# A hand-ordered two-layer Hedgehog attention and ReGLU prompt kernel on one core: a new order, queues for the first loads, transposes in transpose mode, and a last tile split 384 and 128

## The chip, the cores and the metric

The kernel runs on one core of one Trainium2 chip. The metric is the device time of one execution in microseconds (us). Before the change it is 376.75 us, the median of 3 runs (376.38 to 376.97).

Five engines take part, each with its own instruction stream and semaphores between them: TensorE (PE) for matrix products, VectorE (DVE), ScalarE (ACT), GpSimd (POOL), and SyncE (SP), which here only issues DMA transfers. ACT can issue transfers too. An engine takes its own instructions in the order in which they were written down, and stands still when the next one's data are not there.

## The reference

`x` has 2048 rows of 512. Two blocks, A (linear attention, 32 heads of 16) and B (a gated feed-forward of width 1376), are applied twice with the same weights:

```python
def A(x):                                   # B=1, S=2048, D=512, H=32, Dh=16
    q, k, v = split_heads(x @ wqkv)
    pq, pk = q @ w_phi, k @ w_phi           # per head, 16x16
    phi_q = concat(softmax(pq), softmax(-pq))
    phi_k = concat(softmax(pk), softmax(-pk))
    kv, z = phi_k.T @ v, phi_k.sum(over s)
    o = (phi_q @ kv) / (phi_q @ z + 1e-6)
    return merge_heads(o) @ wo
def B(x):
    gate, up = x @ W_gate, x @ W_up
    return (relu(gate) * up) @ W_down
x = x + A(layernorm(x)); x = x + B(layernorm(x))     # twice
```

Everything is bfloat16 outside, with 32-bit sums inside.

## The kernel before

The 2048 rows are 16 tiles of 128. `w_phi` is folded into the key and query weights at the start: a weight is turned on PE (`turn`, L444) or by DMA (L439), multiplied by a block-diagonal matrix (`fold`, L452), and cast back to SBUF (`Wk2`, `Wq2`).

Per tile and layer the attention block does this. `stats` (DVE, L481), `ln` (ACT, L489, function Ln) and `rstd` (ACT, L491, function Exp) make the row scale. The scaled tile is turned, by PE and a cast or by a DMA transpose. `K` (PE, L539) is four products of 128x512 into a PSUM tile `b`, of which there are six. Two `ek` (ACT, L542, Exp) take it out with both signs. `sk` (DVE, L550) sums the heads, `lnk` (ACT, L559, Ln) and `rk` (ACT, L562, Exp) turn the sums into reciprocals, and two `phi` (L513, POOL or DVE) scale. `V` (PE, L545) and its cast `vext` give the values, and `kvz` (PE, L574) adds the tile's part to the sums over all rows. Queries go the same way: `Q` (PE, L601), two `Eq` (ACT, L604, Exp), `sq` (DVE, L607), `lnq` (ACT, L612, Ln), `rq` (ACT, L614, Exp), a scaling, and a DMA transpose `fq`.

When all 16 `kvz` of a layer are in, `R` (DVE, L586 and L591) is built from the sums. Only then can the first `erq` (PE, L638) of the layer run, which makes a tile's attention output; after it come `o`, its turn, `proj` (L661) and the residual. The feed-forward takes blocks of one to four tiles: `G` and `Up` (L738), ACT's relu (L742), the product `hT`, `down` (L778) and the residual (L785). The tail of 96 columns of the width goes through L714. The last tile of layer 1 is stored in two column halves.

The order isn't made by a scheduler on the spot. The program builds 1880 `Op` objects; `ORDER`, a list written out by hand or by a search before, says in which sequence they are emitted, `SLOTS` which buffer each takes, `PLACE` which of two engines an op with an alternative goes to, and `IDLE` how many filler products on zeros stand before which PE op. Each engine's stream is its share of that sequence. `arrange` asserts that an op's `deps` have been emitted before it; what an op has in `follow` is not asserted.

One ACT op matters by its place alone. Op 2, named `tbl`, emits `preload_act_table_set("natural_log_exp_and_others")`: a load of the activation table set that holds both Ln and Exp. No op has it in its `deps`, and it has the load before it in `follow` only. When the program is built, an ACT function that isn't in the set loaded last in the stream gets a load of a set put in before it.

The first transfers of `x` and the weights are bound to a queue in the code, two to ACT and the others to SP. At the very start PE multiplies zeros (`warm`, L423): eight products of 128x512.

Of the kernel before, what the change touches and what calls it, by code (L numbers as in the profile page):

```python
# [8 lines left out]
P = 128  # L9
D = 512  # L10
# [3 lines left out]
NB = D // P  # L14
NF = 11
FR = F - (NF - 1) * P
T = 16
C = 4
# [124 lines left out]
class K:  # L143
# [9 lines left out]
    "0101010100000000001100000001110000101110000110101000000100000101000000010000100000011000000011101010"  # L153
    "1010011010111000101011000001100011100001011100000101101000111000000011000111010011000001101100001011"
    "0110101011100110011100010111110101000100110000001000001100000111100100010000110001001001011010111001"
    "010000101101110101001101111111110"
)
SLOTS = (
    "0011432021055021001401501045313321124221352412451013e0315g31303b0305c12201i012432332391030654220f321"
    "4h220030344d100111082247052a331k1615010b1250052c1344300g0132252j045e363d1200040401141402000224011020"  # L160
    "0400001134021012100000203101002122001002541105001002511102104910002413114215400412511651100100120031"
    "1420302310051535031h432112311505010425412301310405420324310022031410j5100a24022k02327101200410401103"
    "12242250121002352020511310154521505223522020e4231c031213111011021411125513140225000g3420030030020120"
    "03413125121121433231f0121f214i00181651332422193104055j333k204b360a2243033d242h304i113805010401021210"
    "0000121002100010010021140010123402000043001010020111302020011511301002431321101003205504010521311411"
    "5402110501523540013000121032150140030110232043213110025124210401311015522400200403422412313320414041"
    "210100300531330452512524210005215103213300111020141500412"
)
IDLE = (
    0, 0, 0, 1, 0, 0, 0, 0, 0, 0, 1, 0, 1, 0,  # L170
# [105 lines left out]
def kernel(  # L276
# [73 lines left out]
    def load_x(t, n, due, follow=(), eng="SP"):  # L350
        o = load(due, X[t // C][:, t % C:t % C + n, :], xv[:, t:t + n, :], n * 131072, eng, follow)
        x_in[t:t + n] = [o] * n
# [438 lines left out]
    p = PAR  # L791
# [103 lines left out]
```

## Time and profile before

| | |
|---|---|
| time, median of 3 runs | 376.75 us (376.38 to 376.97) |
| the profiled execution's own time | 376.44 us |
| its span, first to last instruction | 374.7 us |
| PE busy | 363.8 us (97%) |
| DVE busy | 275.9 us (74%) |
| ACT busy | 204.3 us (55%) |
| POOL busy | 80.4 us (21%) |
| ACT table loads | 1, of 1283 ns |

The span lies between the first and the last instruction; the execution's own time is 1.7 us longer. "Busy" is the union of an engine's instructions in time. Consecutive ACT instructions overlap, so the step from one start to the next is shorter than an instruction's own duration, and an engine whose instructions start in such steps without a pause has none to spare. Matmuls are pipelined as well.

### The profile page before, as it was taken

To read this page: it belongs to the slowest core of one execution; us is meant where nothing else is said; L and a number is where in the kernel's file an instruction comes from. 1 tells how busy PE (TensorE), PEld (TensorE's weight loads), DVE (VectorE), ACT (ScalarE), POOL (GpSimd) and SP (SyncE) were. 2 spreads that over 40 slices of the span, in tenths; PEclk is the share of its full clock that TensorE was granted. 3 is DMA by queue.
4 is the path that set the end of the run, shared out by engine and by line. 5 is a ranking of instruction groups with operands and counts; after the bars stand their busy time and mean duration, and the time that the engine had idled before them with its cause. 6 is when DMAs were issued, how large, how long until landed. Compare 5 with 4: busy or idle time off the path is not lost.

```text
span 374.7 us, 7403 instructions
## 1 busy us (share of the span) xinstructions
PE 363.8 (97%) x2784; PEld 216.1 (58%) x2830; DVE 275.9 (74%) x587; ACT 204.3 (55%) x561; POOL 80.4 (21%) x93
## 2 busy tenths in 40 slices
PE   7998999999999999999999999999999999999996
PEld 3453455867544544466566456587764444457674
DVE  6999999998775956864789989998776365134333
ACT  5998999655545546344539666874434423313111
POOL 0286985430101100110033533241100000000000
PEclk9999999999999999999999999999999999999999
DMA  8997439875532233042212100488753302020221
GB/s 233 204 232 195 131 81 175 142 142 112 96 59 54 44 65 63 1 84 52 42 38 48 36 0 3 85 115 121 147 94 79 57 0 58 0 56 2 69 74 42
DMA packets 93443, 31.20 MB, mean 83 GB/s; under 512 B 85248, under 2 KB 92384, under 8 KB 93408
## 3 DMA queue, kind: packets, MB, share of 16 engines
q1 hardware_dynamic: 92992, 30.34, 40.1%
q8 instruction: 22, 0.36, 0.4%
q10 hardware_dynamic: 416, 0.39, 0.4%
q14 instruction: 13, 0.11, 0.1%
HBM read 7.91 MB, written 2.10 MB: 27 GB/s over the span
## 4 chain that ended last, share of the span: by engine, by line
PE 89%; issue 1%; ACT 0%; DVE 0%; DVEq 0%
PE b L738 37%; PE b L778 20%; PE b L661 7%; PE b L601 6%; PE b L545 6%; PE b L539 5%; PE b L714 3%; PE q L638 2%; PE q L574 2%; PE b L470 1%; ACT ek L604 0%; DVE o L652 0%; DVE X L785 0%; DVEq L890 0%; ACT lnA L489 0%
## 5 line engine op out<-in xcount | busy, mean ns | idle before, releaser
L738 PE MATMUL b<-xnTB,wgu 128*128 128x128 bf16 (+2 forms) x1200 | 154.5, 279 | 0.2 <-ACT rd L649 0.2
L738 PEld LDWEIGHTS <-wgu 128*128 128x128 bf16 x1200 | 97.5, 98 | 47.3 <-DMA xnTB<-xn 0.4
L742 ACT ACTIVATE gu<-b 128x512 bf16<-128x512 f32 (+1 forms) x83 | 47.2, 581 | 84.8 <-PE b L738 82.0
L778 PE MATMUL b<-wd,hT 128*128 128x512 bf16 (+2 forms) x342 | 83.9, 372 | 0.9
L513 POOL TENSOR_TENSOR ek<-ek,sk 128x512 bf16<-128x512 bf16 x43 | 46.7, 1107 | 122.6 <-ACT sk L562 121.7
L778 PEld LDWEIGHTS <-hT 128*128 128x128 bf16 (+1 forms) x363 | 34.7, 98 | 34.2 <-DVE hT L746 0.2
L755 DVE TENSOR_TENSOR hT<-gu,b 128x512 bf16<-128x512 bf16 (+1 forms) x47 | 30.8, 666 | 30.2 <-ACT gu L742 16.4
L607 DVE TENSOR_REDUCE sq<-ek 128x64 f32<-128x1024 bf16 x32 | 38.4, 1210 | 3.6 <-ACT ek L604 3.5
L604 ACT ACTIVATE ek<-b 128x512 bf16<-128x512 f32 x64 | 37.0, 606 | 6.9 <-PE b L601 6.7
L542 ACT ACTIVATE ek<-b 128x512 bf16<-128x512 f32 x64 | 36.8, 623 | 6.6 <-PE b L539 6.6
L550 DVE TENSOR_REDUCE sk<-ek 128x64 f32<-128x1024 bf16 x32 | 38.2, 1205 | 1.8 <-ACT ek L542 1.8
L785 DVE SCALAR_TENSOR_TENSOR X<-b,rsB,X 128x512 bf16<-128x512 f32 (+1 forms) x33 | 23.9, 729 | 21.2 <-PE b L778 21.0
L757 ACT CAST gu<-b 128x512 bf16<-128x512 f32 (+1 forms) x36 | 20.5, 569 | 25.9 <-PE b L738 25.7
L539 PE MATMUL b<-Wk,xnTA 128*128 128x512 bf16 x122 | 32.2, 379 | 1.1 <-DMA xnTA<-xn 0.6
L545 PE MATMUL b<-wv,xnTA 128*128 128x512 bf16 x124 | 31.8, 379 | 1.3 <-ACT ek L604 1.0
L661 PE MATMUL b<-wo,oT 128*128 128x512 bf16 x121 | 31.5, 379 | 0.4
L622 POOL TENSOR_TENSOR ek<-ek,sq 128x512 bf16<-128x512 bf16 x24 | 25.3, 1060 | 30.4 <-DVE rsB L701 14.3
L601 PE MATMUL b<-Wq,xnTA 128*128 128x512 bf16 x121 | 30.8, 379 | 0.4
L665 DVE SCALAR_TENSOR_TENSOR X<-b,X 128x512 bf16<-128x512 f32 x32 | 22.0, 686 | 9.8 <-PE b L661 9.4
L652 DVE TENSOR_TENSOR o<-q,rd 128x512 bf16<-128x512 f32 x32 | 22.0, 687 | 2.8 <-PE b L738 1.2
L481 DVE BATCH_NORM_STATS2 bstA<-X 128x6 f32<-128x512 bf16 x32 | 21.1, 681 | 2.0 <-DMA X<-in_A_x_dram 1.8
L746 DVE TENSOR_TENSOR hT<-gu 128x512 bf16<-128x512 bf16 (+1 forms) x36 | 15.2, 424 | 10.1 <-ACT gu L757 10.0
(74 smaller groups left out, 351.0 us busy)
## 6 DMA issues: line engine op xcount, KB each, us to landing
out_dram<-X SPq DMA_DIRECT2D x15, 128.0 KB, 1.8
X<-in_A_x_dram SPq DMA_DIRECT2D x6, 256.0 KB, 4.5
wgu<-in_B_W_up_dram SPq DMA_DIRECT2D x4, 344.0 KB, 3.5
wgu<-in_B_W_gate_dram SPq DMA_DIRECT2D x4, 344.0 KB, 4.7
wd<-in_B_W_down_dram SPq DMA_DIRECT2D x5, 256.0 KB, 3.4
wv<-in_A_wqkv_dram SPq DMA_DIRECT2D x2, 256.0 KB, 4.4
wo<-in_A_wo_dram SPq DMA_DIRECT2D x4, 128.0 KB, 3.5
fq<-ek SPq DMA_TRANSPOSE x32, 3.3
```

The source lines that it names most:

```text
L513: e.tensor_tensor(out=out().rearrange("p g s (h f) -> p (g s h) f", f=DH)[:, lo:lo + n], in0=ek.t[:].rearrange("p g s (h f) -> p (g s h) f ...
L539: k = op("PE", mm(4, 512), due, lambda: [nc.tensor.matmul(kp.t[:], lhsT=xnTA[c][:, i, b, :], rhs=Wk2[:, b, :], start=(b == 0), stop=(b == ...
L542: e = [op("ACT", act(512), due, lambda s=s: nc.scalar.activation(out=ek.t[:, :, s, :], in_=kp.t[:].rearrange("p (g e) -> p g e", e=GQ), fu ...
L545: v = op("PE", mm(4, 512), due_v, lambda: [nc.tensor.matmul(vp.t[:], lhsT=xnTA[c][:, i, b, :], rhs=wv[:, b, :], start=(b == 0), stop=(b == ...
L550: a = op("DVE", SUM16, due, lambda: nc.vector.tensor_reduce(out=sk.t[:, row, :], in_=ek.t[:].rearrange("p g s (h f) -> p (g s h) f", f=DH) ...
L601: q = op("PE", mm(4, 512), due, lambda: [nc.tensor.matmul(qp.t[:], lhsT=xnTA[c][:, i, b, :], rhs=Wq2[:, b, :], start=(b == 0), stop=(b == ...
L604: e = [op("ACT", act(512), due, lambda s=s: nc.scalar.activation(out=ek.t[:, :, s, :], in_=qp.t[:].rearrange("p (g e) -> p g e", e=GQ), fu ...
L607: a = op("DVE", SUM16, due, lambda: nc.vector.tensor_reduce(out=sq.t[:], in_=ek.t[:].rearrange("p g s (h f) -> p (g s h) f", f=DH), axis=A ...
L661: a = op("PE", mm(4, 512), due + 3, lambda j=j, yp=yp: [nc.tensor.matmul(yp.t[:], lhsT=oT.t[:, j, b, :], rhs=wo[:, b, :], start=(b == 0), ...
L738: nc.tensor.matmul(ps.t[:, q * W:(q + 1) * W].rearrange("p (i t) -> p i t", t=P), lhsT=wgu[:, s, b, g * P:(g + 1) * P], rhs=xT.t[:, 0:n, b ...
L742: nc.scalar.activation(out=gu.t[:, 0, 0:cols], in_=gp.t[:, 0:cols], func=AF.Relu)
L778: nc.tensor.matmul(yp.t[:, 0:c1 - c0], lhsT=h.t[:m, f * W + i * P:f * W + (i + 1) * P], rhs=wd[:m, f, c0:c1], start=(f == 0), stop=(f == N ...
```

## The change

- `ORDER`, `SLOTS`, `PLACE` and `IDLE` are new throughout. `IDLE` has two filler products, not three.
- `warm` is seven zero products, not eight.
- The loads of `x`, of the key and value weights and of `w_phi` get an alternative: ACT or SP may issue them, as `PLACE` says. ACT now issues five, SP 28 of the loads (before: two and 31).
- The turns on PE, which were products with the identity into 32-bit PSUM, are transposes (`nc.tensor.transpose`) into the same PSUM tile read as bfloat16; the cast that takes them out reads bfloat16.
- The last tile of layer 1 is split into 384 and 128 columns, not 256 and 256.

```diff
-    0, 0, 0, 1, 0, 0, 0, 0, 0, 0, 1, 0, 1, 0,
+    0, 0, 0, 2, 0,
...
-    0, 4, 21, 18, 24, 3, 2, 16, 7, 26, 8, 17, 1, 22, 23, 29, 25, 9, 10, 46, 14, 19, 47, 27, 48, 322, 49, 30, 32, 31,
+    16, 7, 8, 17, 29, 24, 18, 22, 4, 3, 21, 19, 23, 20, 26, 322, 0, 1, 10, 324, 64, 82, 65, 323, 83, 66, 27, 30, 67,
...
+    228, 366, 204, 180, 229, 282, 182, 239, 454, 298, 165, 181, 230, 240, 232, 2, 241, 308, 169, 341, 455, 244, 345,
...
-    def load(due, dst, src, nbytes, eng="SP", follow=()):
-        q = nc.sync if eng == "SP" else nc.scalar
-        return op(eng, dma(nbytes), due, lambda: q.dma_start(out=dst, in_=src), name="load", follow=follow,
-                  move=nbytes / RATE)
+    def load(due, dst, src, nbytes, eng="SP", follow=(), both=False):
+        queues = {"SP": nc.sync, "ACT": nc.scalar}
+        ways = {e: (e, dma(nbytes), lambda q=q: q.dma_start(out=dst, in_=src), False) for e, q in queues.items()}
+        return op(eng, dma(nbytes), due, ways[eng][2], name="load", follow=follow, move=nbytes / RATE,
+                  alt=ways["ACT" if eng == "SP" else "SP"] if both else None)
...
-    op("PE", mm(8, 512), 0, lambda: idle(8), [c_z], [wps], name="warm")
+    op("PE", (2570, 2700, 6), 0, lambda: idle(7), [c_z], [wps], name="warm")
...
+    def half(ps):
+        return ps.t[:].bitcast(BF16)[:, 0:NB * P]
...
-        a = op("PE", mm(NB, 128), due, lambda: [nc.tensor.matmul(
-            ps.t[:, b * P:(b + 1) * P], lhsT=src.t[:, 0, b * P:(b + 1) * P], rhs=ident[:], start=True, stop=True)
-            for b in range(NB)], after + [c_id], [ps], [src], name=name)
+        a = op("PE", mm(NB, 128), due, lambda: [nc.tensor.transpose(
+            half(ps)[:, b * P:(b + 1) * P], src.t[:, 0, b * P:(b + 1) * P], ident[:]) for b in range(NB)], after + [c_id], [ps], [src], name=name)
...
-            halves = ((0, 256), (256, 512)) if l == 1 and t == T - 1 else ((0, 512),)
+            halves = ((0, 384), (384, 512)) if l == 1 and t == T - 1 else ((0, 512),)
```

In the list `ORDER`, op 2 (`tbl`) stands at index 6 before and at index 310 after. The ACT stream that is built from the two lists begins like this; the first column is the place in the stream, and lines are those of each kernel's own file (the new file's are two to three higher):

```
before                                            after
1  L346 DMACopy X_61<-in_A_x_dram                 1  L346 DMACopy X_61<-in_A_x_dram
2  L371 LoadActFuncSet                            2  L346 DMACopy hT_162<-in_A_wqkv_dram
3  L346 DMACopy hT_162<-in_A_wqkv_dram            3  L346 DMACopy X_61<-in_A_x_dram
4  L489 Activation lnA_90<-mvA_88,eps             4  L346 DMACopy hT_162<-in_A_wqkv_dram
5  L491 Activation rsA_89<-lnA_90                 5  L346 DMACopy X_62<-in_A_x_dram
6  L429 TensorCopy hT_163<-b_102                  6  L492 LoadActFuncSet
7  L429 TensorCopy hT_163<-b_103                  7  L492 Activation lnA_90<-mvA_88,eps
8  L489 Activation lnA_90<-mvA_88,eps             8  L494 LoadActFuncSet
9  L429 TensorCopy Wk_67<-b_104                   9  L494 Activation rsA_89<-lnA_90
10 L491 Activation rsA_89<-lnA_90                 10 L492 LoadActFuncSet
11 L429 TensorCopy hT_163<-b_105                  11 L492 Activation lnA_90<-mvA_88,eps
12 L429 TensorCopy hT_163<-b_106                  12 L494 LoadActFuncSet
```

Over the whole stream there is 1 `LoadActFuncSet` before and there are 37 after: 36 in front of a Ln or an Exp that is the first or follows one of the other function, and `tbl` itself (L372) at place 143, behind which there is none. Ahead of the first `erq` of layer 0 both PE streams hold the same groups: 16 `K`, 16 `V`, 12 `Q`, 16 `kvz`, four turned tiles, and the turning and folding of the key and query weights. ACT's share ahead of the last `vext` of that layer is the same too, but for three fewer casts of turned tiles (`xnTA`), one fewer of the turned key weight (`wT`), two more of `vext` and one `lnq` fewer; DVE has those turned by ACT before.

More of the change, by code (lines that the diff above doesn't have):

```diff
@@ L152 @@
 PLACE = (
[L153 to L156, printed above, removed]
+    "0010001001000000111010110001000001110000000110000000110000100010000101100010101001000000000000010110"
+    "0101000001110111111111001000010011000001010100001110111011000010011011000110010110101011010110100111"
@@ L157 @@
+    "1101001110110010011001100011000010011111000100101010001000001101010010000001111001000101101100011000"
+    "101111000111110001100001000000001101111110100001"
 )
 SLOTS = (
-    "0011432021055021001401501045313321124221352412451013e0315g31303b0305c12201i012432332391030654220f321"
-    "4h220030344d100111082247052a331k1615010b1250052c1344300g0132252j045e363d1200040401141402000224011020"
-    "0400001134021012100000203101002122001002541105001002511102104910002413114215400412511651100100120031"
@@ L162 @@
[L162 to L166, printed above, removed]
@@ L167 @@
-    "210100300531330452512524210005215103213300111020141500412"
+    "0011432514255040001232121002134310233320053302731103e4125f44110b0334c11110i0305j54121a5200950225h223"
+    "204020413546005k014d1254232834251541365b1133202a061732362402223g011e33091500030401111002000251011020"
+    "1300001130021000330210021402100221010011450404004005114325001c22002012111014324215200h10310500400402"
+    "03045014110422k322504412111115032111121232033043150230033254111530124311284420053302b223001510103000"
+    "21311411232012240050421222251431275105e212226000493210121100100032045243123100a5431g4302050002014122"
@@ L168 @@
+    "1030552124122i23225510013f240i034j365d1523311d24111009035c15432207214434321015060f060j33010302021312"
+    "0000121502100015010021120100202300101130001010230012102025041311501241550401102002201213521421111201"
+    "5502225023512210010004150000051234155245230103004253015143011010104012022415110402015510023324421420"
+    "501400520131330150151330205110114421502011110520250131423"
 )
 IDLE = (
-    0, 0, 0, 1, 0, 0, 0, 0, 0, 0, 1, 0, 1, 0,
+    0, 0, 0, 2, 0,
 )
@@ L341, in op @@
         return o
-    def load(due, dst, src, nbytes, eng="SP", follow=()):
-        q = nc.sync if eng == "SP" else nc.scalar
-        return op(eng, dma(nbytes), due, lambda: q.dma_start(out=dst, in_=src), name="load", follow=follow,
-                  move=nbytes / RATE)
+    def load(due, dst, src, nbytes, eng="SP", follow=(), both=False):
[3 more added lines that the diff above has]
+                  alt=ways["ACT" if eng == "SP" else "SP"] if both else None)
     wqkv = A_wqkv.rearrange("(b p) f -> p b f", p=P)
     def load_x(t, n, due, follow=(), eng="SP"):
-        o = load(due, X[t // C][:, t % C:t % C + n, :], xv[:, t:t + n, :], n * 131072, eng, follow)
+        o = load(due, X[t // C][:, t % C:t % C + n, :], xv[:, t:t + n, :], n * 131072, eng, follow, True)
         x_in[t:t + n] = [o] * n
@@ L361, in w_load @@
     def w_load(w, k, b, eng):
-        return lambda f: load(b, w[:, b:b + 2, :], wqkv[:, b:b + 2, k * D:(k + 1) * D], 262144, eng, f)
+        return lambda f: load(b, w[:, b:b + 2, :], wqkv[:, b:b + 2, k * D:(k + 1) * D], 262144, eng, f, True)
     def first_x(t, n, eng="SP"):
@@ L374 @@
         w_load(wk, 1, 0, "SP"),
-        lambda f: load(2, wf[:], A_w_phi.rearrange("(b j) d f -> (j d) b f", b=NB, j=8), 65536, "SP", f),
+        lambda f: load(2, wf[:], A_w_phi.rearrange("(b j) d f -> (j d) b f", b=NB, j=8), 65536, "SP", f, True),
         w_load(wv, 2, 0, "SP"), w_load(wv, 2, 2, "SP"), first_x(1, 1), first_x(2, 1), first_x(3, 1), first_x(4, 2),
@@ L423, in idle, with evac @@
             nc.tensor.matmul(wps.t[:, 0:NB, :], lhsT=zero[:, 0:P], rhs=zero[:], start=True, stop=True)
-    op("PE", mm(8, 512), 0, lambda: idle(8), [c_z], [wps], name="warm")
-    def evac(eng, due, out_, in_, deps, takes, uses, name, cols=512):
+    op("PE", (2570, 2700, 6), 0, lambda: idle(7), [c_z], [wps], name="warm")
+    def evac(eng, due, out_, in_, deps, takes, uses, name, cols=512, rate=1):
         both = {"ACT": ("ACT", act(cols), lambda: nc.scalar.copy(out=out_(), in_=in_()), False),
-                "DVE": ("DVE", dve(cols), lambda: nc.vector.tensor_copy(out=out_(), in_=in_()), False)}
+                "DVE": ("DVE", dve(cols, rate), lambda: nc.vector.tensor_copy(out=out_(), in_=in_()), False)}
         _, cost, copy, _ = both[eng]
         return op(eng, cost, due, copy, deps, takes, uses, name=name, alt=both["DVE" if eng == "ACT" else "ACT"])
+    def half(ps):
+        return ps.t[:].bitcast(BF16)[:, 0:NB * P]
     def fold(w, dst, loaded, due, step, engs, by_dma=False):
@@ L443, in fold @@
             ps = Buf(p_b)
-            tr = op("PE", mm(4, 128), due + m, lambda m=m, ps=ps: [nc.tensor.matmul(
-                ps.t[:, b * P:(b + 1) * P], lhsT=w[:, m, b * P:(b + 1) * P], rhs=ident[:], start=True, stop=True)
-                for b in range(NB)], [loaded[m * len(loaded) // NB], c_id], [ps] + ([wT] if m == 0 else []),
+            tr = op("PE", mm(4, 128), due + m, lambda m=m, ps=ps: [nc.tensor.transpose(
+                half(ps)[:, b * P:(b + 1) * P], w[:, m, b * P:(b + 1) * P], ident[:]) for b in range(NB)], [loaded[m * len(loaded) // NB], c_id], [ps] + ([wT] if m == 0 else []),
                 [] if m == 0 else [wT], name="turn")
             turned.append(evac(engs[m % 2], due + m, lambda m=m: wT.t[:, :, m * P:(m + 1) * P],
-                               lambda ps=ps: ps.t[:].rearrange("p (b d) -> p b d", d=P), [tr], (), [ps, wT], "wT"))
+                               lambda ps=ps: half(ps).rearrange("p (b d) -> p b d", d=P), [tr], (), [ps, wT], "wT",
+                               rate=2))
         for m in range(NB):
@@ L469, in turn @@
         ps = Buf(p_b)
-        a = op("PE", mm(NB, 128), due, lambda: [nc.tensor.matmul(
-            ps.t[:, b * P:(b + 1) * P], lhsT=src.t[:, 0, b * P:(b + 1) * P], rhs=ident[:], start=True, stop=True)
-            for b in range(NB)], after + [c_id], [ps], [src], name=name)
-        return evac("ACT", due, lambda: dst()[:, 0], lambda: ps.t[:].rearrange("p (b t) -> p b t", b=NB), [a],
-                    takes, [ps] + uses, name, 512)
+        a = op("PE", mm(NB, 128), due, lambda: [nc.tensor.transpose(
+            half(ps)[:, b * P:(b + 1) * P], src.t[:, 0, b * P:(b + 1) * P], ident[:]) for b in range(NB)], after + [c_id], [ps], [src], name=name)
+        return evac("ACT", due, lambda: dst()[:, 0], lambda: half(ps).rearrange("p (b t) -> p b t", b=NB), [a],
+                    takes, [ps] + uses, name, 512, 2)
     def nothing():
```

177 rows, old and new, of the table ORDER are left out of this document.

## The prediction

> **What bounds the kernel now.** I read the page first, for the bound over the whole span; then busy time by stretches, because that share is a mean over stages; then ACT's own waits and its timeline, because the new order puts 36 more instructions there.
>
> ```profile
> span 374.7 us, 7403 instructions
> PE 363.8 (97%) x2784; PEld 216.1 (58%) x2830; DVE 275.9 (74%) x587; ACT 204.3 (55%) x561; POOL 80.4 (21%) x93
> PEclk9999999999999999999999999999999999999999
> PE 89%; issue 1%; ACT 0%; DVE 0%; DVEq 0%
> ```
>
> Over the span PE is the bound, and the chain that ended last runs through it for 89%. ACT's 55% looks like room. The stretches say where that room is not:
>
> ```profile
> 30.00:40.00 10.00, 8.90 (x55) 4.19 (x55) 10.00 (x14) 9.97 (x31) 7.68 (x8) 1.00 0.67 162
> 40.00:50.00 10.00, 9.95 (x61) 4.81 (x61) 10.00 (x11) 10.00 (x31) 9.86 (x11) 1.00 0.44 124
> ...
> 100.00:120.00 20.00, 19.89 (x118) 9.80 (x118) 12.78 (x35) 11.38 (x32) 0.00 (x0) 1.00 0.38 64
> ...
> 3.94:54.24 50.30, 47.27 (x347) 24.38 (x352) 48.95 (x82) 46.07 (x138) 31.31 (x30) 1.00 0.79 191
> 56.30:374.65 318.35, 312.59 (x2412) 189.89 (x2450) 223.06 (x491) 154.91 (x419) 46.41 (x55) 1.00 0.35 66
> ```
>
> The columns are the stretch and its length, then PE, PEld, DVE, ACT and POOL, each busy time with its count of instructions. From 30 to 50 us PE, DVE and ACT are full together; from 100 on ACT has two fifths to spare. So ACT has no room in the attention of layer 0. How little, its waits up to 54.3 us tell:
>
> ```profile
> ACT lnA L489 <- DVE mvA L482: 3.6, 2, 2.1
> ACT hT L429 <- PE b L444: 1.7, 1, 1.7
> ACT L371 <- PEq L879: 1.2, 1, 1.2
> ACT sk L559 <- DVE sk L550: 0.3, 1, 0.3
> ```
>
> Without the waits ahead of its first Ln (1.5 of the first row, and the third row), ACT waits 2.1 + 1.7 + 0.3 = 4.1 us. This is its timeline at the start, and at the end of the stretch, with what PE does there:
>
> ```profile
> 1.19 1.28 ACT L371 ACT_TABLE_LOAD   x1 [1.19 <-PEq L879]
> 1.22 0.47 ACTq L346 DMA_DIRECT2D hT<-in_A_wqkv_dram  x1
> 3.94 0.29 ACT L489 ACTIVATE lnA<-mvA,eps 128x1 f32<-128x1 f32 x1 [1.46 <-DVE mvA L482]
> 4.26 0.20 ACT L491 ACTIVATE rsA<-lnA 128x1 f32<-128x1 f32 x1
> 6.20 1.07 ACT L429 CAST hT<-b 128x512 bf16<-128x512 f32 x2 [1.74 <-PE b L444]
> ...
> 49.30 0.26 ACT L612 ACTIVATE sq<-sq 128x32 f32<-128x32 f32 x1
> 49.42 0.62 ACT L604 ACTIVATE ek<-b 128x512 bf16<-128x512 f32 x1
> 49.90 0.29 ACT L562 ACTIVATE sk<-sk 128x64 f32<-128x64 f32 x1
> 50.04 0.63 ACT L604 ACTIVATE ek<-b 128x512 bf16<-128x512 f32 x1
> ...
> 53.64 0.60 ACT L429 CAST vext<-b 128x512 bf16<-128x512 f32 x1
> 54.11 0.27 ACT L614 ACTIVATE sq<-sq 128x32 f32<-128x32 f32 x1
> 54.24 0.62 ACT L604 ACTIVATE ek<-b 128x512 bf16<-128x512 f32 x1
> ...
> 54.73 0.67 PE L574 MATMUL q<-vext,ek 128*128 128x65 bf16 x16
> 55.46 0.81 PE L601 MATMUL b<-Wq,xnTA 128*128 128x512 bf16 x3
> 56.30 0.42 PE L638 MATMUL q<-R,fq 128*128 128x68 bf16 x8
> ```
>
> Three things are to be seen. A table load takes 1.28 us and holds ACT. ACT's instructions start in steps shorter than they last: 49.42 to 49.90 is 0.48 for one that lasts 0.62, 49.30 to 49.42 is 0.12 for 0.26. And the last `vext` cast (53.64) leads within 1.1 us to the last `kvz` (54.73) and within 2.7 us to the first `erq` (56.30). PE has nothing of the feed-forward to do before that `erq`: it depends on the attention's output.
>
> **The sum.** I measure the change at one place, that first `erq`. Ahead of it both PE streams hold the same groups, so behind it the same PE work is left: 318.35 us of span here. How much later it starts is how much later the kernel ends, as far as the rest keeps its pace.
>
> - *The table.* The preload that serves Ln and Exp moves from third place to place 143 of ACT's stream, and 36 loads come in ahead of it. In the old stream the one load fell into the wait for the first Ln; in the new one the first load may fall there, and the 35 others and `tbl` itself, all ahead of the last `vext`, do not: 36 x 1.283 (the load's 1.28) = 46.2 us.
> - *Lost overlap.* I assume that a load neither starts before the instruction ahead has ended nor lets the next one in early. Then each costs the overlap too, 0.62 - 0.48 or 0.26 - 0.12, that is 0.14: up to 36 x 0.14 = 5.0, and nothing at the least. No row shows an instruction right behind a load.
> - *Waits filled.* Loads can stand where ACT waited: up to 4.1 less, at the least nothing. The wait of 1.74 goes surely, since four loads now stand ahead of the first casts.
> - *Work moved off ACT.* Three casts of turned tiles and one of the key weight go to DVE, two `vext` come: two steps of 0.48 and one `lnq` of 0.12, 1.1 less. DVE, full until now, gains room as it waits for ACT.
>
> The sum has its ends at 46.2 - 1.1 - 4.1 = 41.0 and 46.2 - 1.1 + 5.0 = 50.1. I take 45: three quarters of the waits filled (3.1) and three fifths of the overlap lost (3.0). It is nearer the middle than an end, because a load is an instruction in the same queue (overlap lost) and waits in front of a slower ACT shrink.
>
> Behind each load stand the exps and casts that free the six PSUM tiles `b`, so PE's next K, V or Q waits for them; and `lnk` and `rk`, for which the scaling on POOL and DVE waits and after it `kvz`. That is late next.
>
> **The other edits**, with their cover:
>
> ```profile
> 1.96 3.59 PE L423 MATMUL q<-zero 128*128 128x512 bf16 x8 [1.96 <-DVE zero L394]
> 5.57 0.82 PE L444 MATMUL b<-ident,hT 128*128 128x128 bf16 x8
> 6.23 0.38 PE L423 MATMUL q<-zero 128*128 128x512 bf16 x1
> ...
> L430 DVE CAST vext<-b 128x512 bf16<-128x512 f32 x7 | 4.8, 681 | 0.4 <-ACT sq L612 0.4
> L746 DVE TENSOR_TENSOR hT<-gu 128x512 bf16<-128x512 bf16 x33 | 13.8, 420 | 9.5 <-ACT gu L757 9.5
> L785 DVE SCALAR_TENSOR_TENSOR X<-b,rsB,X 128x256 bf16<-128x256 f32 x2 | 0.9, 480 | 0.6 <-PE b L778 0.6
> L785 DVE SCALAR_TENSOR_TENSOR X<-b,rsB,X 128x512 bf16<-128x512 f32 x31 | 23.0, 746 | 20.6 <-PE b L778 20.4
> ```
>
> Seven zero products end about 0.4 us sooner, in front of the turn that waits for its weight (5.57): nothing, and at most 0.4 either way. One filler less is 0.2 us of PE in a stage where PE will wait: nothing. Three more loads issued by ACT take some 0.47 each (the row at 1.22), and the key weight's second half is now ACT's fourth; the first casts are late by the loads anyway, so nothing, and without that cover 1.4. Transposes stream as many columns as the products did. Their casts read 16 bits, which no row shows from PSUM: between 420 ns (L746, from SBUF) and 681 (L430) on DVE, hidden behind ACT in layer 0; the few behind it could give 0.3 each. For the last tile, the final residual of 128 columns costs less than the 480 ns of 256: 746 less 480 is 266 for 256 columns more, so some 0.35; but the 384 columns ahead of it cost 0.6, as much more. Nothing, with bounds of -0.2 and +0.2.
>
> What the new order does behind 56.3 us the old trace can't show. PE stands idle for 318.35 - 312.59 = 5.8 us there, so it can't gain more than that; I take zero, and as much for a loss.
>
> The profiled execution took 376.44 us, 1.7 more than its span and 0.3 less than the median. 376.4 + 45 = 421.4; I say 421.5. Its own range is 411.6 to 432.3: the sum's ends with 5.8 taken off and put on.
>
> **A rule on the price.** The trace bounds a switch from above as well: between the load's end (2.47) and the Ln at 3.94 lie 1.46 us, put down to DVE, so a switch could hold ACT for 1.28 + 1.46 without this trace telling. The Trainium skill, page "ScalarE: Activation LUTs", section "What ACT_TABLE_LOAD costs", gives 1283 ns for the load, which the row shows, and adds about 1380 ns of drain to each switch, which no row here shows. By the load alone and no other correction the end is 376.4 + 46.2 = 422.6; by the page's 2.66 us a switch it would be an estimated 376.4 + 36 x 2.66 = 472.
>
> **The rivals.**
>
> - *Every switch also stops ACT for as long as that gap.* For it: nothing in the trace excludes it. Against it: the Ln at 3.94 follows DVE's row statistics, and so explains the gap. Then 36 x 1.46 = 52.6 come on top, in place of the lost overlap of 3.0: 421.5 + 49.6 = 471. I give it 0.09.
> - *PE falls to half pace in the gaps.* The eight zero products took 3.59 us, 0.45 each, while a single one at 6.23 lasts 0.38 with its start-up and three Q products at 55.46 took 0.81 (0.22 a step): PE starts at half pace here, though the clock row says full. Waiting for ACT, it could go back. Its 47.3 us of the stretch would become 94.5, about as long as ACT's 50.3 + 45 = 95.3, and each would wait for the other. If a third of the 28 K and Q groups that ACT waits for came 0.86 (four steps) late, that is 8 more: 429.5. The Trainium skill, "TensorE: Matmul & The Clock Gate", Part 1, says the clock halves only after a whole window of about 3.4 us without work, which a PE fed every 2 or 3 us avoids; by it the sum stands. I give 0.06.
> - *Not slower: a later load costs next to nothing.* The only load shown is the first of the program; one that goes back to a set used before might cost no more than a small instruction, the 0.12 of the step at 49.30. 36 x 0.12 = 4.3 less 4.1 of waits and 1.1 of moved work is -0.9: 375.5. It decides from (4.1 + 1.1)/36 = 0.14 us a load downwards. Against it: the row says 1283 ns, and nothing ties it to being first. 0.03.
>
> **How the numbers follow.** The sum has 0.82, the rivals 0.09, 0.06 and 0.03. For 8 in 10 I take 411 to 436: the sum's own range and the half-pace case; the long switch, the cheap load and the sum's outermost ends are left out. Only the cheap load ends at or below today's time: faster by over 0.2% (about what a measurement of this kernel tells from no change) 0.02, within 0.2% 0.01, slower 0.97.
>
> **What would show it.** In the new profile: 37 rows of ACT_TABLE_LOAD, 36 ahead of ACT's place 143, near 1283 ns each; ACT full from about 4 to 100 us, while PE's busy tenths fall to about five there; the first L641 (the old L638) at about 101 us instead of 56.3; PE full behind it, with about 318 us from there to the end. The sum is wrong if that `erq` starts before 97 or after 107, if the step from an instruction before a load to the one behind it is far from 1.3 to 1.45 us more than without, or if the length behind the `erq` isn't within 6 us of 318. If PE's L539 products take 0.43 us a step between 10 and 90 us, the half-pace rival holds.

## The result, and the profile after

| | before | after |
|---|---|---|
| time, median | 376.59 us (376.38 to 376.97, 4 runs) | 426.2 us (425.45 to 426.79, 4 runs) |
| ratio | | 1.1315, 95% interval 1.1294 to 1.1336 |
| span of the profiled execution | 374.7 us | 424.4 us |
| first `erq` of layer 0 starts | 56.30 us | 105.99 us |
| from there to the end of the span | 318.35 us | 318.4 us |

The page of the changed kernel, in the lines that answer to those of before: busy times, granted clock, and the chain that ended last.

```profile
span 424.4 us, 7469 instructions
PE 383.1 (90%) x2828; PEld 221.4 (52%) x2828; DVE 271.3 (64%) x581; ACT 255.7 (60%) x601; POOL 82.6 (19%) x98
PEclk8588887769999999999999999999999999999999
PE 73%; ACT 20%; DVE 3%; DMA 2%; issue 1%; ACTq 0%; DVEq 0%
```

ACT now holds a fifth of the chain, where it had nothing; its busy time is 51 us longer. The clock row shows that PE's clock is below full in the first nine slices of 10.6 us and full ever after.

Stretches of ten us ahead of the first `erq`, then from the first Ln up to it, and from it to the end (columns as in the prediction: PE, PEld, DVE, ACT, POOL, then granted clock, DMA share, GB/s):

```profile
20.00:30.00 10.00, 6.40 (x29) 2.63 (x27) 4.37 (x11) 9.88 (x16) 0.00 (x0) 0.84 0.44 116
60.00:70.00 10.00, 5.48 (x27) 2.16 (x26) 2.96 (x4) 9.86 (x15) 2.45 (x3) 0.84 0.07 14
...
6.81:103.40 96.59, 61.98 (x331) 29.07 (x332) 47.06 (x76) 94.41 (x169) 28.55 (x28) 0.77 0.35 94
106.00:424.40 318.40, 314.32 (x2451) 189.39 (x2450) 218.71 (x485) 157.38 (x426) 52.21 (x63) 1.00 0.35 66
```

ACT is full. PE, which was full beside it before, stands idle for a third to a half of these stretches, and DVE for half of them and more. Behind the `erq` nothing has changed: PE is full again, for the same length. ACT's waits up to 104 us, and ACT's timeline at the start, in the middle and at the last `vext` cast:

```profile
ACT L492 <- DMA hT<-in_A_wqkv_dram: 5.5, 1, 5.5
ACT sq L615 <- DVE sq L610: 0.4, 1, 0.4
ACT sk L562 <- DVE sk L553: 0.3, 1, 0.3
ACT Wk L430 <- PE b L456: 0.2, 1, 0.2
ACT Wq L430 <- PE b L456: 0.2, 1, 0.2
```

```profile
2.25 0.46 ACTq L346 DMA_DIRECT2D hT<-in_A_wqkv_dram  x1
5.11 0.37 ACTq L346 DMA_DIRECT2D X<-in_A_x_dram  x1
5.52 1.28 ACT L492 ACT_TABLE_LOAD   x1 [5.52 <-DMA hT<-in_A_wqkv_dram]
6.81 0.29 ACT L492 ACTIVATE lnA<-mvA,eps 128x1 f32<-128x1 f32 x1
7.12 1.28 ACT L494 ACT_TABLE_LOAD   x1
8.42 0.20 ACT L494 ACTIVATE rsA<-lnA 128x1 f32<-128x1 f32 x1
...
42.42 1.06 ACT L545 ACTIVATE ek<-b 128x512 bf16<-128x512 f32 x2
43.51 1.28 ACT L562 ACT_TABLE_LOAD   x1
44.80 0.40 ACT L562 ACTIVATE sk<-sk 128x64 f32<-128x64 f32 x2
...
103.33 0.57 ACT L430 CAST vext<-b 128x512 bf16<-128x512 f32 x1
103.80 0.61 ACT L607 ACTIVATE ek<-b 128x512 bf16<-128x512 f32 x1
...
105.99 0.42 PE L641 MATMUL q<-R,fq 128*128 128x68 bf16 x8
```

A load begins 0.03 us behind the end of the instruction ahead (42.42 + 1.06 = 43.48, then 43.51), and the next instruction 0.01 behind the load (43.51 + 1.28, then 44.80). So it is around every load: but for the wait ahead of the first, the gaps ahead are 0.03 us at most, those behind 0.01 or 0.02. No instruction overlaps a load, and none is held longer. `tbl` itself, the last load, starts at 93.26; counted as in the listing, with the five transfers, it has place 148 of ACT's stream (2 before), and 143 without them. Within the stretch ACT waits 1.1 us where it waited 4.1. But the first Ln starts at 6.81 instead of 3.94: ACT's fifth transfer isn't issued before 5.11, and the first load stands behind it in ACT's queue.

### The profile page after: what moved, and what is told of

Its sections match the earlier page's. It is cut to its first block, busy times and chain, and to the rows that moved or that the text cites. A ratio compares the mean times of both kernels' runs of the same rounds, so it can differ in the third digit from the quotient of the medians.

```text
span 424.4 us, 7469 instructions
## 1 busy us (share of the span) xinstructions
PE 383.1 (90%) x2828; PEld 221.4 (52%) x2828; DVE 271.3 (64%) x581; ACT 255.7 (60%) x601; POOL 82.6 (19%) x98
## 4 chain that ended last, share of the span: by engine, by line
PE 73%; ACT 20%; DVE 3%; DMA 2%; issue 1%; ACTq 0%; DVEq 0%
PE b L741 31%; PE b L781 18%; PE b L664 7%; PE b L604 4%; ACT ek L545 4%; PE b L548 3%; PE b L542 3%; ACT L492 3%; PE b L717 3%; ACT L562 2%; ACT L494 2%; PE q L641 2%; ACT L565 2%; ACT L545 2%; PE q L577 1%
## 5 line engine op out<-in xcount | busy, mean ns | idle before, releaser
L741 PE MATMUL b<-xnTB,wgu 128*128 128x128 bf16 (+2 forms) x1200 | 152.4, 280 | 0.0
L781 PE MATMUL b<-wd,hT 128*128 128x512 bf16 (+3 forms) x363 | 85.2, 373 | 0.0
L516 POOL TENSOR_TENSOR ek<-ek,sk 128x512 bf16<-128x512 bf16 x48 | 51.4, 1090 | 135.9 <-ACT sk L565 133.6
L542 PE MATMUL b<-Wk,xnTA 128*128 128x512 bf16 x128 | 37.6, 428 | 16.5 <-ACT ek L545 6.6
L758 DVE TENSOR_TENSOR hT<-gu,b 128x512 bf16<-128x512 bf16 (+1 forms) x44 | 29.1, 663 | 29.2 <-PE b L741 15.9
L548 PE MATMUL b<-wv,xnTA 128*128 128x512 bf16 x128 | 38.0, 434 | 6.2 <-ACT vext L430 2.7
L604 PE MATMUL b<-Wq,xnTA 128*128 128x512 bf16 x128 | 33.5, 391 | 3.1 <-ACT ek L545 3.1
L502 DVE TENSOR_SCALAR xn<-X,mvA,rsA 128x512 bf16<-128x512 bf16 x32 | 13.8, 452 | 32.6 <-ACT rsA L494 32.6
L788 DVE SCALAR_TENSOR_TENSOR X<-b,rsB,X 128x512 bf16<-128x512 f32 (+2 forms) x33 | 23.3, 726 | 13.6 <-PE b L781 13.5
L542 PEld LDWEIGHTS <-xnTA 128*128 128x128 bf16 x128 | 13.1, 106 | 33.5 <-issue 20.5
```

Source lines behind the costliest of these rows:

```text
L516: e.tensor_tensor(out=out().rearrange("p g s (h f) -> p (g s h) f", f=DH)[:, lo:lo + n], in0=ek.t[:].rearrange("p g s (h f) -> p (g s h) f ...
L542: k = op("PE", mm(4, 512), due, lambda: [nc.tensor.matmul(kp.t[:], lhsT=xnTA[c][:, i, b, :], rhs=Wk2[:, b, :], start=(b == 0), stop=(b == ...
L548: v = op("PE", mm(4, 512), due_v, lambda: [nc.tensor.matmul(vp.t[:], lhsT=xnTA[c][:, i, b, :], rhs=wv[:, b, :], start=(b == 0), stop=(b == ...
L604: q = op("PE", mm(4, 512), due, lambda: [nc.tensor.matmul(qp.t[:], lhsT=xnTA[c][:, i, b, :], rhs=Wq2[:, b, :], start=(b == 0), stop=(b == ...
L741: nc.tensor.matmul(ps.t[:, q * W:(q + 1) * W].rearrange("p (i t) -> p i t", t=P), lhsT=wgu[:, s, b, g * P:(g + 1) * P], rhs=xT.t[:, 0:n, b ...
L781: nc.tensor.matmul(yp.t[:, 0:c1 - c0], lhsT=h.t[:m, f * W + i * P:f * W + (i + 1) * P], rhs=wd[:m, f, c0:c1], start=(f == 0), stop=(f == N ...
```

## The experiments

**The table's place, both ways.** The changed kernel with the load of the shared set first:

```diff
+ORDER = tuple([i for i in ORDER if i != 2][:0] + [2] + [i for i in ORDER if i != 2][0:])
```

> The changed kernel with one edit: the load of the set with both Ln and Exp (op 2) is emitted first, not at index 310. Theory (the 36 loads, each 1.28 us and about 0.13 of lost overlap, are the whole loss but for a late first Ln): the 46.8 us by which ACT's stretch grew go, and the first load of 1.3 ahead of the first Ln; the held fifth transfer on ACT stays, so the first Ln comes at about 5.5 us instead of 3.94. 426.2 - 46.8 - 1.3 = 378.1, between 375 and 379; one ACT_TABLE_LOAD. Rival (the new order, the queues or the transposes lose by themselves): above 382.

Measured: 379.56 us, ratio 1.0083 (1.0064 to 1.0102); the `erq` at 59.21. One edit takes 46.6 of the 49.6 us away. It is 0.6 above the range that the theory gave. ACT's timeline shows a likely reason:

```profile
1.19 0.46 ACTq L346 DMA_DIRECT2D hT<-in_A_wqkv_dram  x1
3.40 0.36 ACTq L346 DMA_DIRECT2D X<-in_A_x_dram  x1
5.57 0.44 ACTq L346 DMA_DIRECT2D hT<-in_A_wqkv_dram  x1
7.83 0.37 ACTq L346 DMA_DIRECT2D X<-in_A_x_dram  x1
8.25 0.29 ACT L492 ACTIVATE lnA<-mvA,eps 128x1 f32<-128x1 f32 x1 [6.24 <-DMA hT<-in_A_wqkv_dram]
```

Here three transfers on ACT wait, not one, and the first Ln comes at 8.25. The built streams say for what: in this program each of these transfers signals one of eight completion counts, `DMAHW0` to `DMAHW7`, and a transfer that is dealt a count in use waits until its earlier user has landed.

```
changed kernel, ACT                                 table first, ACT
3 DMACopy X_61<-in_A_x_dram                         4 DMACopy X_61<-in_A_x_dram       [waits DMAHW0]
4 DMACopy hT_162<-in_A_wqkv_dram                    5 DMACopy hT_162<-in_A_wqkv_dram  [waits DMAHW1]
5 DMACopy X_62<-in_A_x_dram [waits DMAHW2]          6 DMACopy X_62<-in_A_x_dram       [waits DMAHW4]
```

How the late start reaches the end isn't settled. PE, which had stood still meanwhile, is full here from 10 to 20 us but at a granted clock of 0.75, and what that adds wasn't tested:

```profile
10.00:20.00 10.00, 9.74 (x76) 7.08 (x75) 7.85 (x23) 8.29 (x21) 0.00 (x0) 0.75 0.58 156
```

The kernel before with that load late:

```diff
+ORDER = tuple([i for i in ORDER if i != 2][:310] + [2] + [i for i in ORDER if i != 2][310:])
```

> The kernel before with one edit: op 2 is emitted at index 310, nothing else is changed. 36 loads come in, one of them in the wait for the first Ln. Theory: 35 x (1.28 + 0.13) = 49.4, less about 3 us of ACT's waits that are filled, on 376.6: 423, between 418 and 427. Rival (a good part of the loss belongs to the rest of the change): below 410.

Measured: 422.44 us, ratio 1.1215 (1.1189 to 1.1242). So the place of one instruction makes 45.7 us in the old order, with the old queues, products and split. The rival that puts a good part of the loss on the rest of the change falls.

**Half of the loads.** The changed kernel with op 2 at index 170 (same edit, 170 for 310): 19 loads.

> The changed kernel with one edit: op 2 at index 170, so that 18 of the 36 loads go (19 in all). Theory (every load ahead of the last vext costs the same, about 1.41 us, and part of the waits come back): 426.2 - 18 x 1.41 + 1.5 = 402.3, between 399 and 405; the first erq at about 82 us. Rival (the loss is made in one place, the loads of the first 25 us or those of the last 20): it stays above 412 or falls below 392.

Measured: 400.71 us, ratio 1.0643 (1.0625 to 1.0662). 426.2 less 400.7 is 25.5 for the 18 later loads: 1.42 each. The first `erq` comes at 81.0, and the rival of one place falls. The earlier loads have no such clean price: from here to the kernel with the table first it is 21.2 us more, but that kernel starts its first Ln later and has some of ACT's waits back.

**Is it the change of set, or the load?** The kernel before with a load of the set that lies there already behind the second exp of each tile's keys in layer 0:

```diff
-                out=ek.t[...], in_=kp.t[...], func=AF.Exp, scale=1.0 - 2.0 * s), [k], ...
+                out=ek.t[...], in_=kp.t[...], func=AF.Exp, scale=1.0 - 2.0 * s)] + (
+                    [nc.scalar.preload_act_table_set("natural_log_exp_and_others")] if s and self.l == 0 else []), [k], ...
```

> The kernel before with 16 more loads of the set that lies there already, one behind the second exp of each tile's keys in layer 0; no function changes its set. Theory (a load costs its 1.28 us and the lost overlap wherever ACT has no room, whether or not the set is new): 376.7 + 16 x 1.41 = 399.3 less up to 4 us of filled waits, between 395 and 400. Rival (a load costs only where it changes the set): 376 to 380.

Measured: 397.29 us, ratio 1.0551 (1.0533 to 1.0569). The group of its loads (busy, mean ns of one, then idle before):

```profile
L543 ACT ACT_TABLE_LOAD x16 | 20.5, 1283 | 0.3
```

20.6 us for 16 loads is 1.29 each, less than 1.41 as it fills waits: ACT's wait of 2.1 us for later row statistics is gone. A load that changes nothing costs what one that changes the set does. The rival "a later load costs next to nothing" falls here too.

**The transfers on ACT.** The changed kernel with its fifth ACT transfer on SP, with the table late and with the table first:

```diff
-    "0010001001000000111010110001000001110000000110000000110000100010000101100010101001000000000000010110"
+    "0010001000000000111010110001000001110000000110000000110000100010000101100010101001000000000000010110"
```

> The changed kernel with one edit: the fifth transfer of ACT's queue (x, tiles 4 and 5), which starts at 5.11 us after a wait and has the first table load behind it, is issued by SP. Theory (its wait holds ACT, and ACT is the bound): the first load starts at about 2.7, the first Ln at about 4.8 and not at 6.81; the end comes 2.0 us sooner, 424.2, between 423.5 and 425. Rival (ACT would have waited for the row statistics or the weights anyway): 426.2.

Measured: 424.79 us, ratio 1.1282 (1.1259 to 1.1305). The first Ln comes at 5.25, 1.6 sooner, and the end 1.4 sooner: nearly all of it reaches the end. (Each of these times is of one execution; with the same start of ACT's stream the first Ln came at 6.31 in the kernel with half of the loads, so 6.81 holds to half a microsecond.)

```profile
2.73 1.28 ACT L492 ACT_TABLE_LOAD   x1 [2.73 <-issue]
5.25 0.29 ACT L492 ACTIVATE lnA<-mvA,eps 128x1 f32<-128x1 f32 x1 [1.24 <-DVE mvA L485]
```

The load now lies in the wait for the row statistics. They come later than in the kernel before (3.94), so 1.3 of the 2.87 us stay.

> The changed kernel with both edits: op 2 first, and the fifth transfer of ACT on SP. Theory: the first Ln comes about 1 us sooner than with the table alone, 1 us less than that run or nothing, 374.5 to 377.5. If the new order is better than the old one where the table doesn't count, it is below 376.

Measured: 378.04 us, ratio 1.0039 (1.0024 to 1.0054), above the expected range by 0.5. Its fourth ACT transfer now waits, until 4.87, and the first Ln comes at 5.31, the `erq` at 56.27, in a profiled execution of 376.97 us that is the fastest of its twelve. With op 2 at index 16 and all first loads on their old queues:

```diff
-    "0010001001000000...
+    "0000000000000000...
+ORDER = tuple([i for i in ORDER if i != 2][:16] + [2] + [i for i in ORDER if i != 2][16:])
```

> The changed kernel with two edits: op 2 at index 16, and the first loads on the queues of the kernel before (ACT issues two, SP the rest), so that no transfer on ACT waits. Theory (what is left of the loss with the table first is transfers that hold ACT at the start): the first Ln by 4.5 us, and 376 to 377.5, less than the 378.0 with the fifth transfer on SP. Rival (the rest of the loss is in the new order behind the start): 378 or more.

Measured: 376.03 us, ratio 0.9986 (0.9971 to 1.0001). The rest of the loss is gone, so it lay in the queues of the first loads and not in the order behind the start. The first Ln came at 4.87, later than expected, and the `erq` at 55.57. By which way the queues cost 2.0 us is shown in part only: between the two profiled executions the first Ln differs by 0.44 us, the `erq` by 0.7 and the end by 1.0. PE's pace may have a share: the granted clock was 0.991 to 0.995 in eleven of the twelve executions with the fifth transfer on SP, and 0.999 or 1.0 in ten of the twelve here. With the old queues, the new order, with the transposes, the seven products and the last tile's split, can't be told from the old kernel.

**Does PE's lower clock cost anything?** The changed kernel with each K group of layer 0 made twice, the second time over the first:

```diff
-                for b in range(NB)], [xT] + k_fold, [kp], name="K")
+                for again in range(2 if self.l == 0 else 1) for b in range(NB)], [xT] + k_fold, [kp], name="K")
```

> The changed kernel with one edit: in layer 0 the four products of each K group are made twice, the second time over the first, so that PE has 16 x 0.86 = 13.8 us more at full pace, 27.5 at half. Theory (ACT sets the end of the stretch; PE's lower granted clock there costs nothing): 426 to 429. Rival (PE at a low clock bounds the stretch too): 436 or more.

Measured: 429.41 us, ratio 1.1406 (1.1383 to 1.1429), 0.4 above the theory's range and 6.6 below the rival's. The stretch, ACT's waits on PE in it, the first `erq`, and PE's longest wait behind it:

```profile
6.81:103.40 96.59, 70.24 (x382) 33.45 (x383) 46.18 (x74) 93.30 (x164) 28.55 (x28) 0.89 0.39 96
...
ACT ek L545 <- PE b L542: 1.1, 1, 1.1
...
106.88 0.41 PE L641 MATMUL q<-R,fq 128*128 128x68 bf16 x8
...
PE q L641 <- DMA fq<-ek: 1.4, 1, 1.4
```

Work of 13.8 us at full pace moved the `erq` by 0.9, or by 1.3 counted from the first Ln (6.35 here), and ACT waited 1.1 for PE. The busier PE had the higher granted clock (0.89 against 0.77), so its busy time in the stretch grew by only 8.3 us, which its idle time took. So PE doesn't set the length of the stretch. What its lower clock costs this run can't say alone, since the clock changed with it; that is bounded by ACT's waits for PE in the changed kernel, 0.4 us. Of the remaining 2.3 us, 1.4 is a wait for a query's transpose in layer 1 that the changed kernel doesn't have; what set that off stays open.

**The small parts**, each alone in the kernel before: the transposes in place of the products with the identity, the last tile's split as in the diff above, and both together with seven zero products.

> The kernel before with the turns on PE as transposes into 16 bits, nothing else. Theory: as many columns are streamed, and the casts cost ACT what they did: within 0.5 us of the kernel before. Rival: 16-bit PSUM is read faster or transposes stall PE: more than 1 us either way.

Measured: 376.78 us, ratio 1.0001 (0.9990 to 1.0012).

> The kernel before with the last tile's columns as 384 and 128, nothing else. Theory: within 0.3 us of the kernel before. Rival: the shorter last residual and store give 0.5 us or more.

Measured: 376.60 us, ratio 0.9998 (0.9987 to 1.0009).

> The kernel before, in its old order, with seven zero products, the transposes and the last tile as 384 and 128: all of the change but the order and the queues. Theory: within 0.7 us of the kernel before.

Measured: 377.14 us, ratio 1.0013 (1.0000 to 1.0025). None does anything that can clearly be told from nothing.

## Why the prediction was right

The forecast was 421.5 us with a range of 411 to 436; the time is 426.2. The mechanism was the one named, at the place named: the first `erq` moved by 49.7 us and the end by as much. By the steps:

- *The same work is left behind the first `erq`*: right, 318.4 us against 318.35.
- *36 loads of 1.28, 46.2 us*: right; 37 loads of 1283 ns, of which one lies ahead of the first Ln.
- *Moved work and filled waits, 1.1 and 3.1 less*: the waits went from 4.1 to 1.1, so 3.0 were filled.
- *Lost overlap, taken as 3.0 of at most 5.0*: too small. From the first Ln to the last `vext` cast ACT needs 103.33 - 6.81 = 96.52, where it needed 53.64 - 3.94 = 49.70. That is 46.8 more; with 46.2 of loads, 1.1 moved and 3.0 filled, what is left for the lost overlap is 4.7 us, 0.13 a load. The gaps around the loads agree: no instruction overlaps one. Taking three fifths had no row behind it.
- *Three more transfers on ACT, "nothing, and without that cover 1.4"*: this step failed. The price was reckoned as three issues of 0.47, hidden by loads that stand ahead of the casts. But the fifth isn't just issued: it waits until 5.11 for a completion count, and the first load and the first Ln, which must precede all else, stand behind it. The first Ln is 6.81 - 3.94 = 2.87 us late. The cover named doesn't exist, since the loads themselves are late. The move to SP gave 1.6 of it back and showed that ACT's start reaches the end nearly in full; the other 1.3 is the row statistics, whose later arrival in the new order the prediction had no term for.
- *From the last cast to the `erq`*: 53.64 to 56.30 before, 103.33 to 105.99 after, 2.66 both times.

The miss of 4.7 us is thus 2.9 for the late first Ln (1.6 the held transfer, 1.3 the statistics) and 1.7 for the overlap, and little else. Both go the same way, so nothing cancelled.

Of the rivals, the long switch would have put 1.46 us between a load and the next instruction; there is 0.01. The 1380 ns of drain that the Trainium skill ("ScalarE: Activation LUTs", "What ACT_TABLE_LOAD costs") adds to a switch do not show here, and the measured price of 1.42 us a load decides. PE's half pace came true as a fact and not as a price: the granted clock was 0.77 in the stretch, yet ACT waited for PE for 0.4 us in all, and doubling the K groups moved the `erq` by only 0.9. The sign that the prediction named for it, K products of 0.43 us a step, is there (four in 1.86 us at 69.95), so that sign was no test of the price. The argument against it, that PE is fed every 2 or 3 us, was wrong: one gap lasted 6 us. The cheap load is refuted by the kernel with 16 loads of the same set.

## What to carry to other kernels

An instruction that nothing depends on can still be what everything relies on; a preload of a table needs an edge to its users, or a search for a better order may move it behind them. An engine's mean share says nothing on what an added instruction costs: ACT was busy 55% of the span and had no room where the loads went. A transfer put on a compute engine's queue costs its issue and, where it has to wait for an earlier one, that wait too, for everything behind it.

## What the runs showed of the hardware

- A load of the set that is there already takes the same 1283 ns as a change of set.
- PE's granted clock fell where PE had little work, and not only after long pauses. PE's products end at 6.18 us and the next start at 12.27. The clock is 1.00 from 6 to 7, 0.81 on the mean from 7 to 8 and 0.50 from 8 on, so it fell at about 7.6, 1.4 us after the last product. It fell again at about 69.1, 0.2 us after a product had ended; the longest pause ahead was 2.53 us there. In the 3 us ahead of each fall PE was busy for about 1 us.

```profile
6.00:7.00 1.00, 0.19 (x1) 0.00 (x0) 0.58 (x1) 0.99 (x2) 0.00 (x0) 1.00 1.26 261
7.00:8.00 1.00, 0.00 (x0) 0.00 (x0) 0.00 (x0) 0.98 (x2) 0.00 (x0) 0.81 1.14 341
8.00:9.00 1.00, 0.00 (x0) 0.00 (x0) 0.00 (x0) 0.97 (x3) 0.00 (x0) 0.50 1.09 303
68.00:69.00 1.00, 0.89 (x4) 0.29 (x3) 1.00 (x2) 1.00 (x1) 0.00 (x0) 1.00 0.00 0
69.00:69.50 0.50, 0.00 (x0) 0.00 (x0) 0.24 (x1) 0.49 (x3) 0.00 (x0) 0.56 0.28 59
```

```profile
5.14 0.62 PE L448 MATMUL b<-ident,hT 128*128 128x128 bf16 x8 [0.79 <-DMA hT<-in_A_wqkv_dram]
5.59 0.59 PE L424 MATMUL q<-zero 128*128 128x512 bf16 x2
12.27 0.61 PE L456 MATMUL b<-Wblk,hT 128*128 128x128 bf16 x4 [6.08 <-ACT hT L430]
...
67.87 1.02 PE L542 MATMUL b<-Wk,xnTA 128*128 128x512 bf16 x4 [2.53 <-ACT vext L430]
69.95 1.86 PE L542 MATMUL b<-Wk,xnTA 128*128 128x512 bf16 x4 [1.06 <-ACT vext L430]
```

The four products of 67.87 take 1.02 us, those of 69.95 take 1.86. "TensorE: Matmul & The Clock Gate" of the Trainium skill, Part 1, has the clock halve after a whole idle window of about 3.4 us. Neither fall had a pause of that length ahead of it, and the measurement decides; two falls give no rule in its place.
